# One matmul of 256 columns for the exponential sums of two heads, and one row buffer for six batches, in a fused attention and expert kernel

## The chip, the cores and the metric

The kernel runs on one core of a Trainium2 chip. A core has a matrix engine (TensorE; PE in the profile, PEld for its loads of stationary weights), a vector engine (VectorE, DVE), a scalar engine (ScalarE, ACT), a general engine (GpSimd, POOL) and an engine that starts transfers (SyncE, SP). They run side by side and wait for each other through semaphores. SBUF is the working memory, PSUM is where TensorE puts its products. The metric is the time of one execution in device microseconds (us).

## The reference

```
scores = scale * q @ k^T                        # 8 batches, 8 heads, 576 tokens, 64 per head
allowed = |i - j| <= 32, or i or j is one of 8 global tokens
attn = exp(scores - max), zero where not allowed
x = (attn / (sum(attn) + 1e-9)) @ v             # 4608 tokens of 512
logits = x @ w_gate                             # 8 experts
e = argmax(logits);  g = softmax(logits)[e]
out = g * (relu(x @ w1[e]) @ w2[e])             # w1 512x1024, w2 1024x512 for each expert
```

All values are fp32; the kernel multiplies fp16 values where it can and adds in fp32.

## The kernel before, in words

The attention part is a loop over 8 batches (`b`) of 6 stages (`t`), 48 in all, written out in full. A stage takes 48 keys of each half of the sequence (`f`, 0 and 1), and the 8 global keys, against the queries in their windows; a row of scores has 128 columns (`WE`). Heads come in 4 pairs (`c`), with a head `r` in each.

The order of the work is written by hand (a manual schedule): each engine executes its instructions in the order of the program. In a stage stand, in this order: transposes of the next batch's keys (`trans_qk`); `scores` of the next stage (L419 to L441) and their exponentials on ACT (`exps`, L445); a piece of the tail of the batch before; `pvs`, the products of exponentials with values (L456); transposes of the next queries; `zs`, the sums of exponentials (L461 to L471). `zs` multiplies a column selector `onesel` with the exponentials: for each of 2 heads, 4 pairs and 2 halves one fp32 matmul of 128 columns, the second head adding to the first in PSUM, in a different row of the same 32.

What is in PSUM is merged over the stages into `xt` (values) and `zt` (sums) by `merge` (L473 to L493): ACT copies the new columns (L486), DVE adds the overlapping ones (L491, or copies them at the first stage, L489). At a batch's end POOL joins the two halves (`join`, L501 to L506; DVE does it for the last batch), and `sum_globals` (L508 to L516) adds up the columns of global queries on POOL.

A `Tail` then turns a batch into routed rows. Its steps are spread over the stages of the next batch: `gate` multiplies `xt` by the gate's weights (L544) and adds the sums from `zt` into free rows of the same PSUM result, with a floor of 1e-30 (L548); `logits` transposes (L559), takes reciprocals of the sums and normalises (L564 to L571); `rows` transposes `xt` (L580) and multiplies it by the reciprocals into an fp16 row buffer `x16` (L581); `route1`, `ranks`, `route2` choose experts and slots; `exps` and `weights` write token numbers (L623, ACT) and gate weights (L659, DVE) to the last four columns of each row; `scatter` (L664) sends six groups of 108 rows from POOL, by indirect DMA, to slots in DRAM. The scatters of batch `b` are issued in batch `b + 2`, one after each stage. The row buffers are two, used by even and odd batches: one carved from the later home of the expert weights (`wall`), one a tile of its own (`x16x`).

At the top of batches 1 to 6 POOL also casts the next keys and queries (L328, eight casts), and fills global keys. During the last batch, rows of the first batches are gathered for the first two experts, whose first wave of matmuls (L769, L776) is interleaved with the last tail. The second part goes through the 8 experts with weights loaded through SP (L679), casts on ACT and DVE (L684, L686), and matmuls (L1155, L1176).

PSUM buffers named `tr` are two, shared by transposes, gates, logits and rows; `sc`, `pv` and `z` have one each.

Of the kernel before, what the change touches and what calls it, by code (L numbers as in the profile page):

```python
# [9 lines left out]
FP32 = mybir.dt.float32  # L10
FP16 = mybir.dt.float16
I32 = mybir.dt.int32
I16 = mybir.dt.int16
ALU = mybir.AluOpType
AF = mybir.ActivationFunctionType
AX = mybir.AxisListType
# [5 lines left out]
B, H, S, D = 8, 8, 576, 64  # L22
NG = 8
NTOK, DM, E, F = 4608, 512, 8, 1024
HW = 48
NSL = 12
NT = 6
KU = HW + NG
R = 6
WP = 20  # L30
WQ = R * WP
WE = WQ + NG
QP = 108
XP = 60
TB = 108
# [4 lines left out]
ROW = DM + 4  # L40
# [5 lines left out]
def kernel(  # L46
# [11 lines left out]
    nc = tc.nc  # L58
# [13 lines left out]
    def carve(parts, ncols, dt):  # L72
        n16 = ncols * (2 if dt is FP32 else 1)
        a = carve_at[0]
        carve_at[0] = a + (n16 + 15) // 16 * 16
        assert carve_at[0] <= 8 * 8192
        r = wflat[0:parts, a : a + n16]
        return r.bitcast(FP32) if dt is FP32 else r
# [4 lines left out]
    vb = [carve(128, NT * DM, FP32).rearrange("p (t n) -> p t n", t=NT) for _ in range(2)]  # L83
# [14 lines left out]
        r = stage[a // 1024][0:parts, a % 1024 : a % 1024 + n]  # L98
        return r.rearrange("p (a b) -> p a b", b=shape[1]) if len(shape) > 1 and parts == 128 else r

    x16b = [carve(TB, 6 * ROW, FP16).rearrange("p (j n) -> p j n", j=6)]

    att = ExitStack()
    ap_ = att.enter_context(tc.tile_pool(name="att", bufs=1))
# [3 lines left out]
    pvp = aps.enter_context(tc.tile_pool(name="ps_pv", bufs=1, space=PS))  # L108
    trp = aps.enter_context(tc.tile_pool(name="ps_tr", bufs=2, space=PS))

    x16b.append(ap_.tile([TB, 6, ROW], FP16, name="x16x"))

    xt = [ap_.tile([128, 2, 4, R + 1, XP], FP32, name=f"xt{i}") for i in range(2)]
    zt = [ap_.tile([128, 2, R + 1, XP], FP32, name=f"zt{i}") for i in range(2)]
    gsum = ap_.tile([128, 5, HW], FP32, name="gsum")
    xtg = ap_.tile([128, 5, B * NG], FP32, name="xtg")
    qt = [ap_.tile([128, 4, R, QP], FP16, name=f"qt{i}") for i in range(2)]
    kt = [ap_.tile([128, 4, NSL, 64], FP16, name=f"kt{i}") for i in range(2)]
    mask = carve(128, NSL * WE, FP16).rearrange("p (n w) -> p n w", n=NSL)
# [9 lines left out]
    id32 = sb.tile([128, 128], FP32, name="id32")  # L129
    idh = sb.tile([128, 128], FP16, name="idh")  # L130
    id2 = ap_.tile([128, 64], FP16, name="id2")
    onesel = ap_.tile([128, 2, 32], FP32, name="onesel")
    wgbd = ap_.tile([128, 4, 32], FP32, name="wgbd")
    ustr = ap_.tile([TB, 128], FP16, name="ustr")
    ones16 = ap_.tile([TB, 128], FP16, name="ones16")
# [132 lines left out]
    for a in (0, 64):  # L268
        s_ = slice(a, a + 64)
# [22 lines left out]
    for dst, src in ((kgh, k), (qgh, q)):  # L292
        for r in range(2):
# [4 lines left out]
                            in1=hsel.rearrange("p (h o) -> p h o", o=1).to_broadcast([64, H, 64]), op=ALU.mult)  # L298
# [14 lines left out]
    for eng, t0, t1 in ((nc.vector, 0, 1), (nc.gpsimd, 1, NT)):  # L313
        for f in range(2):
            ts = slice(NT * f + t0, NT * f + t1)
            eng.tensor_tensor(out=mask[:, ts, NG:WE], in0=m1o[:, :, NG:WE].to_broadcast([128, t1 - t0, WQ]),
                              in1=gk[:, ts].rearrange("p (n o) -> p n o", o=1).to_broadcast([128, t1 - t0, WQ]), op=ALU.add)
# [54 lines left out]
    for r in range(2):  # L372
        nc.sync.dma_start(
            out=wgbd[64 * r : 64 * r + 64, :, 8 * r : 8 * r + 8],
            in_=moe_w_gate.rearrange("(c r p) e -> r p c e", c=4, r=2)[r])
# [1 line left out]
    nc.vector.memset(qt[1][:, :, :, 102:108], 0.0)  # L377
    nc.vector.memset(kt[1][:, :, :, KU:64], 0.0)
    nc.vector.memset(onesel, 0.0)
    nc.vector.memset(onesel[:, 0, 16:17], 1.0)  # L380
    nc.vector.memset(onesel[:, 1, 17:18], 1.0)


    def routing_constants():
# [76 lines left out]
    def zs(b, t):  # L461
        e = eb[(NT * b + t) % 2]
        z = pvp.tile([128, 2, 512], FP32, tag="z", name="z")
        for r in range(2):
            for c in range(4):
                for f in range(2):
                    ff = slice(64 * f, 64 * f + KU)
                    nc.tensor.matmul(out=z[32 * c : 32 * c + 32, f, 0:WE],  # L468
                                     lhsT=onesel[ff, r, :], rhs=e[ff, r, c, :],
                                     start=(r == 0), stop=(r == 1))  # L470
        return z  # L471

    def merge(t, parts):  # L473

        o = 8 * t
        new, old = [], []
        for src, acc in parts:

            sn = bass.AP(src.tensor, src.offset, [list(src.ap[0]), list(src.ap[1]), [WP, R + 1], [1, 8]])
            new.append((acc[:, :, :, o + 12 : o + WP], sn))
            old.append((acc[:, :, 1 : R + 1, o : o + 12],
                        src[:, :, NG:WE].rearrange("p n (r a) -> p n r a", r=R)[:, :, :, 0:12]))
        def part(i):
            nc.scalar.activation(out=new[i][0], in_=new[i][1], func=AF.Copy)  # L486
            d_, s_ = old[-1 - i]
            if t == 0:
                nc.vector.tensor_copy(d_, s_)  # L489
            else:  # L490
                nc.vector.tensor_tensor(out=d_, in0=d_, in1=s_, op=ALU.add)  # L491

        return part  # L493

    def merge_x(b, t, pv):
        return merge(t, [(pv[:, f].rearrange("p (c w) -> p c w", c=4), xt[b % 2][:, f]) for f in range(2)])

    def merge_z(b, t, z):
        merge(t, [(z[:, :, 0:WE], zt[b % 2])])(0)

    def join(b, eng):  # L501
        x, z = xt[b % 2], zt[b % 2]
        for f, a0, a1 in ((0, 48, 0), (1, 6, 54)):
            for y in ((x[:, f, :, 1:, a0 : a0 + 6], x[:, 1 - f, :, 1:, a1 : a1 + 6]),
                      (z[:, f, 1:, a0 : a0 + 6], z[:, 1 - f, 1:, a1 : a1 + 6])):
                eng.tensor_tensor(out=y[0], in0=y[0], in1=y[1], op=ALU.add)  # L506

    def sum_globals(b):  # L508
        x, z = xt[b % 2], zt[b % 2]
        for y, g, d in ((x[:, :, :, 0, 12:XP], gsum[:, 0:4], xtg[:, 0:4]), (z[:, :, 0, 12:XP], gsum[:, 4], xtg[:, 4])):  # L510

            nc.gpsimd.tensor_tensor(out=g, in0=y[:, 0], in1=y[:, 1], op=ALU.add)
            for i, (n, m) in enumerate(((0, 24), (0, 8), (0, 16))):
                w = 24 if i == 0 else 8
                o = g[..., 0:w] if i < 2 else d[..., 8 * b : 8 * b + 8]
                nc.gpsimd.tensor_tensor(out=o, in0=g[..., 0:w], in1=g[..., m : m + w], op=ALU.add)  # L516
# [4 lines left out]
    class Tail:  # L521
        def __init__(self, b):
            self.b = b
            self.glob = b == B
            self.nj = 1 if self.glob else 6
            self.np = 64 if self.glob else TB
            self.lg = ap2.tile([TB, 6, 8], FP32, tag="lg", name="lg")
            self.rz = ap2.tile([TB, 6, 8], FP32, tag="rz", name="rz")
            self.x16 = x16b[b % 2]
            self.lsb = {}  # L530

        def xap(self, c, i):
            if self.glob:
                return xtg[:, c : c + 1, :]
            x = xt[self.b % 2][:, :, c] if c < 4 else zt[self.b % 2]
            o = (2 * i + 1) * XP + 6
            return x.rearrange("p f r a -> p f (r a)")[:, :, o : o + TB]

        def gate(self, i):
            nf = 1 if self.glob else 2  # L540
            n = nf * self.np
            ps = trp.tile([128, 512], FP32, tag="tr", name="tr_l")
            for c in range(4):
                nc.tensor.matmul(out=ps[32 * c : 32 * c + 32, 0:n].rearrange("p (f w) -> p f w", f=nf),  # L544
                                 lhsT=wgbd[:, c, :], rhs=self.xap(c, i), start=True, stop=True)
            l = ap2.tile([128, 2, TB], FP32, tag=f"lsb{i % 2}", name="lsb")

            nc.vector.scalar_tensor_tensor(out=l[:, 0:nf, 0 : self.np], in0=self.xap(4, i), scalar=1e-30,  # L548
                                           in1=ps[:, 0:n].rearrange("p (f w) -> p f w", f=nf),
                                           op0=ALU.max, op1=ALU.add)  # L550
            self.lsb[i] = l

        def logits(self, i):
# [234 lines left out]
    ps = trp.tile([128, 512], FP32, tag="tr", name="tr_v")  # L788
# [9 lines left out]
    for b in range(B):  # L798
# [9 lines left out]
        if b:  # L808
            sum_globals(b - 1)
# [3 lines left out]
        for t in range(NT):  # L813
            n = NT * b + t
# [13 lines left out]
            elif b + 1 == B:  # L828
# [6 lines left out]
                elif t == 5:  # L835
                    for i in range(2 * NW):
                        ps = trp.tile([128, 4, 128], FP16, tag="tr", name="tr_w")
# [36 lines left out]
            elif b + 1 == B and t == 1:  # L874
                tail.logits(1)
            mx(1)
            z = zs(b, t)
            merge_z(b, t, z)
            if b + 1 == B:
                if t == 0:  # L880
# [26 lines left out]
            elif t == 3:  # L907
                for s_ in range(2):
                    nc.sync.dma_start(out=vg.rearrange("p (u s r) d -> p u s (r d)", u=2, s=2)[8:64, :, s_],
                                      in_=vgr[64 * s_ + 8 : 64 * s_ + 64].rearrange("p (u r) d -> p u (r d)", u=2))  # L910
# [13 lines left out]
            if b + 1 == B and t < 2 * NW:  # L924
                gather(xr01[t], wi[:, t // 2, t % 2 : t % 2 + 1], scattered[0 : 6 * (B - 3)])
            if done is not None:
                done.scatter([t])
            if b + 1 == B and t >= 4:
                tail.scatter([t - 4])
            for _ in range(2 if n + 2 == NT * B else 1):  # L930
# [3 lines left out]
            if n >= NT * B - 18 and pre:  # L934
                staged.append((pre.pop(0), stage[len(pre) % 4]))
                wload(*staged[-1][0], staged[-1][1])
        join(b, nc.gpsimd if b + 1 < B else nc.vector)
        done = tail
        tail = Tail(b)
    tg = Tail(B)  # L940
    sum_globals(B - 1)
    assert not staged
    done.scatter([2, 3, 4, 5])
# [196 lines left out]
    for e in range(E):  # L1140
# [11 lines left out]
        for fb in range(8):  # L1152
            ps = psh.tile([128, 512], FP32, tag="h", name="h")[:, 0:N]
            for c in range(4):
                nc.tensor.matmul(out=ps, lhsT=w1v[:, e, c, 128 * fb : 128 * fb + 128], rhs=xts[:, c, 0:N],  # L1155
                                 start=(c == 0), stop=(c == 3))
# [3 lines left out]
            if fb % 2:  # L1160
                castp(nc.scalar if fb % 4 == 1 else nc.vector)
                j = fb // 2
# [10 lines left out]
        for j in range(NJ[e]):  # L1173
            ps = psy.tile([128, 512], FP32, tag="y", name="yp")
            for fc in range(8):
                nc.tensor.matmul(out=ps, lhsT=ht[:, fc, 128 * j : 128 * j + 128], rhs=w2v[:, e, fc, :],  # L1176
                                 start=(fc == 0), stop=(fc == 7))
# [111 lines left out]
```

## Time and profile before

| | us |
|---|---|
| median of 14 runs | 514.81 |
| lowest and highest | 508.63, 519.22 |
| the profiled execution | 517.26 |
| its span, first to last instruction | 515.5 |
| last z group of the attention part ends (span time) | 306.8 |

A line of a group reads: source line, engine, operation, what it writes from what, shape, count, then busy time, mean duration of one in ns, and idle time of the engine just before with what ended it. "Issue" means that the profile shows nothing that the engine waited for. In rows of a stretch, each engine has its busy time in us and, in brackets, how many instructions were in flight; the granted clock of TensorE, the busy share of the DMA engines and GB/s follow.

### The profile page before, as it was taken

Reading aid. Unit: us, or ns where it says so; the run is one execution under the profiler, and the core shown is the slowest. Engines: PE = TensorE matmul, PEld = TensorE weight load, DVE = VectorE, ACT = ScalarE, POOL = GpSimd, SP = SyncE. Lnnn points to the kernel's source line nnn. Section 1 sums busy time; section 2 is a strip of 40 time slices with the busy share of each in tenths; the row PEclk is TensorE's granted clock in tenths of the full one; section 3 lists DMA queues with packets and bytes.
Section 4 is the critical chain, followed back from the end, with each engine's and each line's share of the span. In section 5 each row is a group of like instructions: output and inputs, shape, how many; then the busy total and the mean of one; then the engine's idle time right before and its main releaser. Section 6 shows DMA issues by size and latency. Waiting matters only on the chain.

```text
span 515.5 us, 16371 instructions
## 1 busy us (share of the span) xinstructions
PE 419.7 (81%) x6661; PEld 260.1 (50%) x6661; DVE 253.8 (49%) x719; ACT 211.6 (41%) x385; POOL 241.3 (47%) x387
## 2 busy tenths in 40 slices
PE   3788779978797799797897857577989998999990
PEld 2456557746465476474574534345434444444450
DVE  6533445735355266376484427325775554333330
ACT  7234344523344155274472452234445544323330
POOL 7700370844806606518238134657436556543442
PEclk9999988978879779897598679879899999999997
DMA  8795979773914925947344201379989999221011
GB/s 200 107 212 104 218 159 186 157 169 55 245 46 102 207 49 111 301 135 168 118 126 138 67 24 39 102 253 308 355 246 364 368 366 368 92 79 59 20 42 57
DMA packets 119436, 84.06 MB, mean 163 GB/s; under 512 B 46552, under 2 KB 113880, under 8 KB 119356
## 3 DMA queue, kind: packets, MB, share of 16 engines
q1 hardware_dynamic: 110300, 63.57, 49.1%
q0 software_dynamic: 9056, 19.38, 11.4%
q8 instruction: 55, 0.90, 0.7%
q14 instruction: 25, 0.20, 0.1%
HBM read 68.51 MB, written 16.16 MB: 164 GB/s over the span
## 4 chain that ended last, share of the span: by engine, by line
PE 18%; issue 11%; DMA 9%; DVE 7%; POOL 5%; ACT 3%; another core or an unknown queue 1%; SPq 1%; POOLq 1%; DVEq 0%; ACTq 0%
DMA st<-in_moe_w_dram 6%; PE pv L456 3%; DMA xr<-xslot_scr,ovi 3%; PE yp L1176 3%; POOL xr L691 3%; POOL out_dram L720 2%; PE h L1155 2%; PE hp L769 2%; PE z L468 2%; PE tr_x L580 2%; PE yw L776 1%; ACT wall L684 1%; SPq L679 1%; DVE xt L491 1%
## 5 line engine op out<-in xcount | busy, mean ns | idle before, releaser
L456 PE MATMUL pv<-wall 56*64 56x128 f32 x1536 | 84.5, 323 | 15.3 <-issue 14.1
L456 PEld LDWEIGHTS pv<-wall 56*64 56x64 f32 x1536 | 59.3, 160 | 35.4 <-issue 30.9
L445 ACT ACTIVATE wall<-sc 128x1024 f32<-128x1024 f32 x48 | 49.1, 1023 | 64.0 <-remote 40.4
L506 POOL TENSOR_TENSOR xt<-xt 128x144 f32<-128x144 f32 x14 | 7.1, 506 | 130.4 <-DVE xt L491 130.4
L491 DVE TENSOR_TENSOR xt<-xt,pv 128x288 f32<-128x288 f32 x80 | 36.3, 453 | 62.8 <-ACT xt L486 61.3
L486 ACT ACTIVATE xt<-pv 128x224 f32<-128x224 f32 x96 | 34.3, 357 | 72.1 <-PE pv L456 30.1
L1155 PE MATMUL h<-xts,wall 128*128 128x512 f16 (+1 forms) x256 | 54.1, 354 | 8.7 <-issue 4.9
L1176 PE MATMUL yp<-wall,ht 128*128 128x512 f16 x224 | 51.1, 385 | 0.7 <-DVE ht L733 0.5
L468 PE MATMUL z<-wall,onesel 56*32 56x128 f32 x1536 | 41.9, 312 | 3.8 <-issue 3.7
L720 POOL DMA_INDIRECT out_dram<-y,xr x24 | 25.2, 1052 | 35.4 <-DVE y L717 23.2
L1155 PEld LDWEIGHTS <-wall 128*128 128x128 f16 x256 | 24.3, 98 | 29.9 <-issue 9.3
L328 POOL CAST wall<-wall 96x768 f16<-96x768 f32 (+1 forms) x48 | 37.3, 821 | 0.0
L438 PEld LDWEIGHTS <-kt 64*64 64x64 f16 x1536 | 28.6, 123 | 14.0 <-issue 10.7
L1176 PEld LDWEIGHTS <-ht 128*128 128x128 f16 x224 | 21.8, 99 | 26.6 <-issue 1.5
L580 PE MATMUL tr_x<-id,xt 128*108 128x128 f32 x192 | 32.1, 297 | 3.5 <-DVE x16x L581 1.8
L684 ACT ACTIVATE wall<-st 128x1024 f16<-128x1024 f32 x24 | 25.3, 1053 | 20.7 <-DMA st<-in_moe_w_dram 14.2
L664 POOL DMA_INDIRECT xslot_scr<-wall,si x25 | 24.8, 992 | 18.6 <-ACT wall L445 10.0
L468 PEld LDWEIGHTS z<-wall,onesel 56*32 56x32 f32 x1536 | 23.9, 119 | 16.4 <-issue 12.3
L438 PE MATMUL sc<-qt,kt 64*64 64x120 f16 x768 | 28.4, 238 | 3.5 <-issue 3.5
L733 DVE TENSOR_SCALAR ht<-h 128x512 f16<-128x512 f32 (+1 forms) x32 | 19.9, 622 | 22.3 <-PE h L1155 19.7
L691 POOL DMA_INDIRECT xr<-xslot_scr,idx x24 | 25.4, 1057 | 9.6 <-issue 6.5
L664 POOL DMA_INDIRECT xslot_scr<-x16x,si x24 | 23.9, 996 | 12.4 <-issue 10.6
(270 smaller groups left out, 744.3 us busy)
## 6 DMA issues: line engine op xcount, KB each, us to landing
st<-in_moe_w_dram SPq DMA_DIRECT2D x96, 256.0 KB
wall<-in_v_dram SPq DMA_DIRECT2D x96, 96.0 KB
wall<-in_moe_w_dram SPq DMA_DIRECT2D x32, 256.0 KB
wall<-in_k_dram SPq DMA_DIRECT2D x42, 192.0 KB
wall<-in_q_dram SPq DMA_DIRECT2D x42, 192.0 KB
wall<-vg SPq DMA_DIRECT2D x14, 96.0 KB
wall<-in_k_dram SPq DMA_DIRECT2D x4, 288.0 KB
wall<-in_q_dram SPq DMA_DIRECT2D x4, 288.0 KB
```

Source lines behind the costliest of these rows:

```text
L328: eng.tensor_copy(o, i_)
L438: nc.tensor.matmul(out=o[:, NG:WE].rearrange("p (r a) -> p r a", r=R) if part == 0 else o[:, 0:NG], lhsT=kt[b % 2][rr, c, sl, :], rhs=rhs, ...
L445: nc.scalar.activation(out=e.rearrange("p r c w -> p r (c w)"), in_=sc[:, :, 0 : 4 * WE], func=AF.Exp, scale=0.125)
L456: nc.tensor.matmul(out=pv[64 * r : 64 * r + 64, f, c * WE : (c + 1) * WE], lhsT=vt[ff, t, 64 * h : 64 * h + 64], rhs=e[ff, r, c, :], start ...
L468: nc.tensor.matmul(out=z[32 * c : 32 * c + 32, f, 0:WE], lhsT=onesel[ff, r, :], rhs=e[ff, r, c, :], start=(r == 0), stop=(r == 1))
L491: nc.vector.tensor_tensor(out=d_, in0=d_, in1=s_, op=ALU.add)
L580: nc.tensor.transpose(out=ps[p, 128 * c : 128 * c + 128], in_=src, identity=id32)
L664: d_ = nc.gpsimd.indirect_dma_start(out=xslot, out_offset=IndirectOffsetOnAxis(ap=self.si[p, j : j + 1], axis=0), in_=self.x16[p, j, :].bi ...
L691: d_ = nc.gpsimd.indirect_dma_start(out=xr.bitcast(I16), out_offset=None, in_=xslot, in_offset=IndirectOffsetOnAxis(ap=ix, axis=0), bounds ...
L720: d_ = nc.gpsimd.indirect_dma_start(out=out, out_offset=IndirectOffsetOnAxis(ap=xr[:, DM : DM + 2].bitcast(I32), axis=0), in_=y, in_offset ...
L1155: nc.tensor.matmul(out=ps, lhsT=w1v[:, e, c, 128 * fb : 128 * fb + 128], rhs=xts[:, c, 0:N], start=(c == 0), stop=(c == 3))
L1176: nc.tensor.matmul(out=ps, lhsT=ht[:, fc, 128 * j : 128 * j + 128], rhs=w2v[:, e, fc, :], start=(fc == 0), stop=(fc == 7))
```

## The change

Sums: `zs` has 8 matmuls instead of 16, each over both heads of a pair, 256 columns; `onesel` has ones in both rows 16 and 17, so that both rows get the sums of both heads, each head in columns of its own. `zt`, `gsum` and `xtg` get a dimension for the head. The merge, the join and the sum of globals take both. The gate picks the row that belongs to a head with a mask of rows, `rowsel`, one fused multiply and add for each head; the floor of 1e-30 moves from the gate to the merge.

Row buffers: batches 0 to 5 and 7 share the carved one; batch 6 and the global tokens use the buffer of values that batch 6 leaves free; `x16x` is gone. In batches before the last, the six scatters come after the first four stages.

```diff
-    x16b = [carve(TB, 6 * ROW, FP16).rearrange("p (j n) -> p j n", j=6)]
+    x16b = [carve(TB, 6 * ROW, FP16).rearrange("p (j n) -> p j n", j=6)] * B
+    v16 = vb[B % 2].rearrange("p t n -> p (t n)").bitcast(FP16)[0:TB]
+    x16b[B - 2] = v16[:, 0 : 6 * ROW].rearrange("p (j n) -> p j n", j=6)
+    x16b.append(v16[:, 6 * ROW : 7 * ROW].rearrange("p (j n) -> p j n", j=1))
...
-    x16b.append(ap_.tile([TB, 6, ROW], FP16, name="x16x"))
...
-    zt = [ap_.tile([128, 2, R + 1, XP], FP32, name=f"zt{i}") for i in range(2)]
-    gsum = ap_.tile([128, 5, HW], FP32, name="gsum")
-    xtg = ap_.tile([128, 5, B * NG], FP32, name="xtg")
+    zt = [ap_.tile([128, 2, 2, R + 1, XP], FP32, name=f"zt{i}") for i in range(2)]
+    gsum = ap_.tile([128, 6, HW], FP32, name="gsum")
+    xtg = ap_.tile([128, 6, B * NG], FP32, name="xtg")
...
-    nc.vector.memset(onesel[:, 0, 16:17], 1.0)
-    nc.vector.memset(onesel[:, 1, 17:18], 1.0)
+    nc.vector.memset(onesel[:, 16:18], 1.0)
+
+    for r in range(2):
+        nc.vector.tensor_reduce(out=rowsel[:, r : r + 1], in_=id32.rearrange("p (c n) -> p c n", c=4)[:, :, 16 + r],
+                                op=ALU.add, axis=AX.X)
...
-        for r in range(2):
-            for c in range(4):
-                for f in range(2):
-                    ff = slice(64 * f, 64 * f + KU)
-                    nc.tensor.matmul(out=z[32 * c : 32 * c + 32, f, 0:WE],
-                                     lhsT=onesel[ff, r, :], rhs=e[ff, r, c, :],
-                                     start=(r == 0), stop=(r == 1))
+        for c in range(4):
+            for f in range(2):
+                ff = slice(64 * f, 64 * f + KU)
+                nc.tensor.matmul(out=z[32 * c : 32 * c + 32, f].rearrange("p (r w) -> p r w", r=2)[:, :, 0:WE],
+                                 lhsT=onesel[ff], rhs=e[ff, :, c, :], start=True, stop=True)
...
-            nc.scalar.activation(out=new[i][0], in_=new[i][1], func=AF.Copy)
+            nc.scalar.activation(out=new[i][0], in_=new[i][1], func=AF.Copy, bias=floor)
             d_, s_ = old[-1 - i]
-            if t == 0:
+            if t == 0 and floor:
+                nc.vector.tensor_single_scalar(out=d_, in_=s_, scalar=floor, op=ALU.add)
+            elif t == 0:
                 nc.vector.tensor_copy(d_, s_)
...
-        merge(t, [(z[:, :, 0:WE], zt[b % 2])])(0)
+        merge(t, [(z.rearrange("p f (r w) -> p (f r) w", r=2)[:, :, 0:WE],
+                   zt[b % 2].rearrange("p f r n a -> p (f r) n a"))], 1e-30)(0)
...
-                      (z[:, f, 1:, a0 : a0 + 6], z[:, 1 - f, 1:, a1 : a1 + 6])):
+                      (z[:, f, :, 1:, a0 : a0 + 6], z[:, 1 - f, :, 1:, a1 : a1 + 6])):
...
-            nc.vector.scalar_tensor_tensor(out=l[:, 0:nf, 0 : self.np], in0=self.xap(4, i), scalar=1e-30,
-                                           in1=ps[:, 0:n].rearrange("p (f w) -> p f w", f=nf),
-                                           op0=ALU.max, op1=ALU.add)
+            lv = l[:, 0:nf, 0 : self.np]
+            for r in range(2):
+                nc.vector.scalar_tensor_tensor(out=lv, in0=self.xap(4 + r, i), scalar=rowsel[:, r : r + 1],
+                                               in1=lv if r else ps[:, 0:n].rearrange("p (f w) -> p f w", f=nf),
+                                               op0=ALU.mult, op1=ALU.add)
...
-                done.scatter([t])
+                done.scatter([t] if b + 1 == B else ((0,), (1, 2), (3, 4), (5,), (), ())[t])
```

More of the change, by code (lines that the diff above doesn't have):

```diff
@@ L131 @@
     id2 = ap_.tile([128, 64], FP16, name="id2")
-    onesel = ap_.tile([128, 2, 32], FP32, name="onesel")
+    onesel = ap_.tile([128, 32], FP32, name="onesel")
+    rowsel = ap_.tile([128, 2], FP32, name="rowsel")
     wgbd = ap_.tile([128, 4, 32], FP32, name="wgbd")
@@ L463, in zs, with merge @@
         z = pvp.tile([128, 2, 512], FP32, tag="z", name="z")
-        for r in range(2):
-            for c in range(4):
-                for f in range(2):
-                    ff = slice(64 * f, 64 * f + KU)
-                    nc.tensor.matmul(out=z[32 * c : 32 * c + 32, f, 0:WE],
-                                     lhsT=onesel[ff, r, :], rhs=e[ff, r, c, :],
-                                     start=(r == 0), stop=(r == 1))
+        for c in range(4):
[3 more added lines that the diff above has]
+                                 lhsT=onesel[ff], rhs=e[ff, :, c, :], start=True, stop=True)
         return z
-    def merge(t, parts):
+    def merge(t, parts, floor=0.0):
         o = 8 * t
@@ L509, in sum_globals @@
         x, z = xt[b % 2], zt[b % 2]
-        for y, g, d in ((x[:, :, :, 0, 12:XP], gsum[:, 0:4], xtg[:, 0:4]), (z[:, :, 0, 12:XP], gsum[:, 4], xtg[:, 4])):
+        for y, g, d in ((x[:, :, :, 0, 12:XP], gsum[:, 0:4], xtg[:, 0:4]), (z[:, :, :, 0, 12:XP], gsum[:, 4:6], xtg[:, 4:6])):
             nc.gpsimd.tensor_tensor(out=g, in0=y[:, 0], in1=y[:, 1], op=ALU.add)
@@ L528, in __init__ @@
             self.rz = ap2.tile([TB, 6, 8], FP32, tag="rz", name="rz")
-            self.x16 = x16b[b % 2]
+            self.x16 = x16b[b]
             self.lsb = {}
@@ L534, in xap @@
                 return xtg[:, c : c + 1, :]
-            x = xt[self.b % 2][:, :, c] if c < 4 else zt[self.b % 2]
+            x = xt[self.b % 2][:, :, c] if c < 4 else zt[self.b % 2][:, :, c - 4]
             o = (2 * i + 1) * XP + 6
```

## The prediction

> **What bounds the kernel now.** I read the page first, then the groups with their shapes kept apart, then busy time by stretches, then the timeline of single stages. The page has TensorE (PE) busy for most of the span:
>
> ```profile
> PE 419.7 (81%) x6661; PEld 260.1 (50%) x6661; DVE 253.8 (49%) x719; ACT 211.6 (41%) x385; POOL 241.3 (47%) x387
> ```
>
> That share mixes three regimes of the attention part (0 to 307 us), which the stretches keep apart (columns: PE, weight load, DVE, ACT, POOL, granted clock, DMA share, GB/s):
>
> ```profile
> 98.00:102.00 4.00, 3.91 (x140) 2.83 (x118) 3.30 (x11) 2.54 (x5) 3.61 (x10) 1.00 1.02 249
> 105.00:110.00 5.00, 2.51 (x21) 1.28 (x20) 0.00 (x0) 0.95 (x1) 3.78 (x5) 0.85 1.13 252
> 196.00:200.00 4.00, 4.00 (x120) 2.96 (x124) 3.13 (x9) 2.11 (x5) 2.75 (x6) 1.00 0.43 76
> 210.00:215.00 5.00, 2.53 (x21) 1.13 (x20) 0.00 (x0) 0.00 (x0) 3.96 (x4) 0.93 1.16 290
> 282.00:287.00 5.00, 2.67 (x13) 0.83 (x14) 0.00 (x0) 0.00 (x0) 3.06 (x4) 0.50 0.30 84
> ```
>
> Normal stages take about 4 us (from one L468 group to the next in the timeline: 191.36, 195.28, 199.20, 203.29, 207.27), with 120 to 140 matmuls in 4 us: PE is the bound there. The rows with 13 to 21 matmuls in 5 us are the second regime: POOL issues six row scatters (L664) one after another, 1.3 us apart, and PE trickles without any semaphore being named. It costs about 7 us in each of batches 2 to 6 and more in batch 7, and lasts as long as POOL's scatters do (208.73 to 216.22 in batch 5; PE is back at 217.4). The third is batch 0, where PE waits for DVE's casts.
>
> What is to change stands in these groups (line, engine, operation, names, shape, count | busy us, mean ns | idle before):
>
> ```profile
> L468 PE MATMUL z<-wall,onesel 56*32 56x128 f32 x1536 | 41.9, 312 | 3.8 <-issue 3.7
> ...
> L486 ACT ACTIVATE zt<-z 128x112 f32<-128x112 f32 x48 | 12.5, 260 | 10.1 <-remote 6.5 <-PE z L468 3.5
> L491 DVE TENSOR_TENSOR zt<-zt,z 128x144 f32<-128x144 f32 x40 | 11.9, 298 | 7.9 <-ACT zt L486 4.6 <-issue 3.3
> ...
> L548 DVE SCALAR_TENSOR_TENSOR lsb<-zt,tr_l 128x216 f32<-128x216 f32 x24 | 8.9, 373 | 10.2 <-PE tr_l L544 10.2
> ```
>
> How matmuls of one such group follow each other is seen by cutting one group of 32 into four slices; the count beside PE is of matmuls in flight in the slice (columns: PE, weight load, DVE, ACT, clock, DMA, GB/s):
>
> ```profile
> 199.19:199.30 0.11, 0.10 (x8) 0.10 (x16) 0.00 (x0) 0.00 (x0) 1.00 0.17 19
> 199.32:199.41 0.09, 0.09 (x16) 0.09 (x21) 0.00 (x0) 0.00 (x0) 1.00 0.21 23
> 199.43:199.52 0.09, 0.09 (x24) 0.09 (x16) 0.00 (x0) 0.00 (x0) 1.00 0.21 23
> 199.54:199.63 0.09, 0.09 (x25) 0.06 (x8) 0.00 (x0) 0.00 (x0) 1.00 0.21 23
> ```
>
> Eight start together (eight corners of the array: two row halves, four column strips), then eight more about every 0.11 us: four rounds, two heads times the two passes that a fp32 product takes here. Within a round starts are 7 ns apart, so a round is set by its 128 columns, not by the number of instructions. The same stage on the other engines:
>
> ```profile
> 199.20 0.67 PE L468 MATMUL z<-wall,onesel 56*32 56x128 f32 x32
> ...
> 199.67 0.37 DVE L548 SCALAR_TENSOR_TENSOR lsb<-zt,tr_l 128x216 f32<-128x216 f32 x1
> ...
> 200.55 0.30 DVE L489 COPY zt<-z 128x144 f32<-128x144 f32 x1
> ...
> 200.76 0.37 DVE L548 SCALAR_TENSOR_TENSOR lsb<-zt,tr_l 128x216 f32<-128x216 f32 x1
> ...
> 201.31 0.39 PE L544 MATMUL tr_l<-xt,wgbd 128*32 128x216 f32 x4
> ```
>
> **The change, part by part.**
>
> *Z matmuls.* Per stage 16 fp32 products of 128 columns become 8 of 256; in records 32 become 16, and 1536 of 13,322 PE records (matmuls and weight loads) disappear. The columns streamed through each corner are the same: four rounds of 0.11 us become two of 0.21 to 0.22 us (L544 shows it: 216 columns, second pass 0.21 us after the first). The last instruction starts earlier and lasts about 0.11 us longer, so the group still takes about 0.66 against 0.67 us. I take 0. From both sides: all the overhead of the three round changes gone, 0.03 us x 48 = -1.4 us; no overlap between the two wider rounds, 0.03 x 48 = +1.4 us. [...]
>
> *PE's supply of instructions.* Fewer instructions help where PE is starved. In batch 7 the z group itself lies in a scatter stretch (279.5 to 287.7): 64 records in 8.2 us. The stretch ends with POOL, so the saved slots only let PE do some 30 later instructions early, worth about 0.4 us at normal speed. PE also stops once for 2.6 us in the middle of L438 (163.8 to 166.4) with no wait named, while a 16 KB packet of the instruction queue arrives; all such stops on L438 add to 6.3 us, longest 2.6. A tenth fewer instructions: 0.6 us. Together -1.0; bounds -6.3 (none left) and +2.6 (they fall elsewhere, one more long one).
>
> *Evacuation of z.* ACT's copy goes from 112 to 224 elements: the row for that size is L486 xt, 357 ns, +0.10 us; DVE's from 144 to 288: L491 xt, 453 ns, +0.155 us. Times 48 that is 4.7 us of ACT and 7.4 us of DVE. ACT's (41% busy) is covered by PE's stage, except in batch 0; without the cover it costs up to 4.7. DVE's lands on PE in two places. Batch 0: PE waits for a DVE cast in four stages, and that cast stands behind zt, which stands behind ACT's zt: 4 x 0.25 = +1.0. In batches 1 to 6, the transpose group L580 at 193.67 waits 0.3 us for DVE's row product (L581), which stands behind zt: 6 x 0.155 = +0.9. Elsewhere DVE has about a quarter of each normal stage free (3.13 of 4.00 busy); if not, 48 x 0.155 = 7.4. [...]
>
> *Gate.* One fused operation becomes two, the second waiting for the first. Price of the second: 373 ns by L548 itself; its operands are all in SBUF, where L506 on DVE (144 elements) plus 72 elements at L491's slope gives 375; with 35 ns between dependent operations 0.41 us, x 24 = 9.8 us, plus 0.25 for the global tail (its row is 209 ns). The tr buffer is released by the first of the two. In the timeline above the next gate's matmul (201.31) needs the buffer that L548 releases at 201.13: with a second operation and a longer zt ahead of it, less 0.14 us idle, that moves by some 0.4, slack 0.18: about +0.2 in each of batches 1 to 6, +1.2. In batch 7 gates and logits stand close together (268 to 276, DVE nearly always busy, PE waits for `tmp`): +0.8. In the last tail (309.8 to 316) DVE gets up to 0.86 us late but PE's interleaved expert matmuls cover most: +0.4. Bound: all on the path, 10.1.
>
> *POOL.* The z part of the join grows from 36 to 72 elements (262 ns; between that and 506 for 144, about 343), twice, and of the global sums by about 0.2: scatters start 0.35 us later per batch. PE is then starved later by as much and no longer: 0, at most 5 x 0.35 = 1.8.
>
> *One row buffer.* Scatters 1 to 5 stand earlier in POOL's program (after stages 0 to 3 rather than 0 to 5), six indirect DMAs as before, past no other POOL work in batches 2 to 6 and past nothing on SP. POOL reaches them late anyway (208.7, when PE is in stage 2), so they issue at the same times. New waits: DVE's row products in stage 3 for scatter 0, ACT's token write L623 in stage 4 for all six; behind the first DVE's merges queue, behind the second ACT's next exponentials, and PE behind both. In batch 5 the last scatter is issued by 216.2 and its queue is empty at 220.1; ACT comes to L623 at 224.7. Margin 4.6 us: cost 0. Rows in `wall` also make L623 wait for DVE (3 waits, 3.2 us; none in x16x) and now do so in each batch; stages with it are as long as those without (3.93, 3.92): 0, at most 3 x 1.05. The row mask (two small reductions for one memset less) lies in the setup, under loads: 0, at most 0.5.
>
> Sum: 0 - 1.0 + 1.0 + 0.9 + 1.2 + 0.8 + 0.4 = +3.3 us. The profiled execution took 517.26 us (span 515.5) and would be 520.6; the median of the 14 runs is 514.81, which makes 518.1.
>
> **The rivals.**
> A, faster: the starved stretches cost per instruction and not per scatter. Then batch 7's z group loses half of its 8.2 us (-4.1), the 2.6 us stop goes, and half of the DVE cost hides (+2.2): 514.8 - 4.5 = 510.3. For it: matmuls at a steady 4 per us there. Against: PE recovers within about 1.5 us of POOL's last scatter, in every batch.
> B, no change: DVE's idle quarter takes all of it; +4.3 goes, -1.0 stays: 513.8. For it: PE is rarely seen waiting for DVE. Against: the two places where it is.
> C, much slower: the single buffer makes ACT wait in stage 4. It decides once POOL is 4.6 us later than now; at 6 us it costs 1.4 in each of five batches, 518.1 + 7 = 525. For it: POOL is a chain from the join through eight casts. Against: 0.35 us is all that is added.
> That the change saves PE nothing is part of my forecast.
>
> **How the numbers follow.** Forecast 0.56, own range 515.5 to 520.5; A 0.16; B 0.18; C 0.10. About 0.5% (2.6 us) is what a measurement of this kernel can tell: faster is under 512.2, slower over 517.4. Faster: nearly all of A, 0.16. Slower: two thirds of the forecast (0.38) and C, 0.48. Within: B and the rest, 0.36. The range reaches from the upper part of A to the lower part of C, 511.5 to 523.5.
>
> **What would show it.** Right: L468 with 768 records, one group still 0.6 to 0.7 us; ACT zt near 357 and DVE zt near 453 ns; two L548-like operations near 370; normal stages 4.0 to 4.2 us, longer in stages 1 and 5; scatter stretches as long as before. Wrong: z groups near 0.4 us (the columns do not bind), shorter scatter stretches (A), ACT waiting for a scatter's DMA in stage 4 (C).

## The result, and the profile after

The changed kernel takes **532.93 us** (median of 10 runs, 522.59 to 538.3) against 514.78 us for the kernel before beside it (47 runs), 18 us more. The ratio, 1.023 (95% interval 1.018 to 1.028) or 12 us, compares only the fast runs of each kernel, those within 1.5% of its fastest. So it is slower, as forecast, but by 12 to 18 us and not by 3.3, and above the upper end of the range. The profiled execution has a span of 529.8 us against 515.5.

The page of the changed kernel, busy time by engine:

```profile
PE 423.7 (80%) x5893; PEld 248.6 (47%) x5893; DVE 284.1 (54%) x745; ACT 215.5 (41%) x385; POOL 247.7 (47%) x387
```

PE has 768 records fewer and is no less busy; ACT has 4 us more, POOL 6 us more and DVE 30 us more. The groups of the changed kernel, shapes apart (busy us, mean ns | idle before), say where these 30 us are:

```profile
L474 PE MATMUL z<-wall,onesel 56*32 56x256 f32 x768 | 40.3, 469 | 0.3 <-issue 0.2
...
L558 DVE SCALAR_TENSOR_TENSOR lsb<-zt,rowsel,lsb 128x216 f32<-128x216 f32 x24 | 24.5, 1021 | 0.8
...
L499 DVE TENSOR_TENSOR zt<-zt,z 128x288 f32<-128x288 f32 x40 | 18.0, 450 | 15.3 <-ACT zt L492 12.2 <-issue 3.0
...
L492 ACT ACTIVATE zt<-z 128x224 f32<-128x224 f32 x48 | 17.0, 354 | 17.1 <-remote 9.3 <-PE z L474 6.2 <-PE tr_qk L345 1.2
...
L558 DVE SCALAR_TENSOR_TENSOR lsb<-zt,rowsel,tr_l 128x216 f32<-128x216 f32 x24 | 10.3, 429 | 1.8 <-PE tr_l L553 1.7
```

The sums (L474) and their evacuation (L492, L499) cost what the prediction says. The surprise is the second operation at the gate, the one whose two tensor inputs are `zt` and `lsb`: 1021 ns in the mean, where 0.41 us was priced. The same line of the trace by itself shows that this is no mean of equal pieces (ns min/median/max, first and last start), and who waited for it (us, times):

```profile
L558 DVE SCALAR_TENSOR_TENSOR lsb<-zt,rowsel,tr_l x24: 421/428/440, 63.6 to 326.0; 128x216 f32<-128x216 f32 x24
L558 DVE SCALAR_TENSOR_TENSOR lsb<-zt,rowsel,lsb x24: 444/556/3127, 64.1 to 326.5; 128x216 f32<-128x216 f32 x24
...
  PE tr_l L553: 11.7, 5
```

The first operation, which reads `tr_l` from PSUM, is the same everywhere. The second is 444 ns where it is short and 3127 ns where it is long. The timeline of batch 5 (start us, us) shows what lies beside a long one:

```profile
204.27 5.59 POOL L332 CAST wall<-wall 96x768 f16<-96x768 f32 x7
...
205.09 0.43 DVE L558 SCALAR_TENSOR_TENSOR lsb<-zt,rowsel,tr_l 128x216 f32<-128x216 f32 x1
...
205.55 2.85 DVE L558 SCALAR_TENSOR_TENSOR lsb<-zt,rowsel,lsb 128x216 f32<-128x216 f32 x1
...
208.32 0.44 DVE L497 COPY xt<-pv 128x288 f32<-128x288 f32 x1
208.69 0.44 DVE L495 TENSOR_SCALAR zt<-z 128x288 f32<-128x288 f32 x1
...
209.06 0.42 DVE L558 SCALAR_TENSOR_TENSOR lsb<-zt,rowsel,tr_l 128x216 f32<-128x216 f32 x1
```

POOL runs its casts of the next batch's queries and keys back to back, and the operation lasts until five of them are over. Behind it on DVE stand the merge of `xt`, that of `zt` and the next gate's first operation, and PE waits 2.73 us for a `tr` buffer. The stretches of the changed kernel (length, then PE, weight load, DVE, ACT, POOL, granted clock, DMA share, GB/s) show what this costs PE:

```profile
205.00:207.00 2.00, 1.80 (x66) 0.95 (x50) 1.96 (x3) 1.32 (x4) 2.00 (x4) 1.00 0.39 45
207.00:209.00 2.00, 0.00 (x0) 0.00 (x0) 2.00 (x3) 0.96 (x1) 2.00 (x3) 0.86 0.48 137
209.00:211.00 2.00, 1.47 (x20) 0.79 (x24) 1.50 (x4) 0.00 (x0) 2.00 (x4) 0.50 1.02 272
211.00:213.00 2.00, 2.00 (x34) 1.55 (x26) 0.56 (x2) 0.36 (x1) 1.76 (x6) 0.50 1.15 248
213.00:215.00 2.00, 2.00 (x26) 1.05 (x24) 1.48 (x4) 0.71 (x2) 1.15 (x6) 0.50 1.18 248
```

The kernel before, in the same stages of its own batch 5:

```profile
205.00:207.00 2.00, 1.91 (x73) 1.46 (x62) 1.73 (x6) 1.41 (x3) 1.76 (x6) 1.00 1.15 243
207.00:209.00 2.00, 2.00 (x66) 1.39 (x67) 1.56 (x5) 1.15 (x4) 1.13 (x5) 1.00 1.20 237
```

After the change PE does nothing from 207 to 209 us, and then the clock granted to it is half until 215: 20 to 34 matmuls in 2 us instead of 66 to 73 at full clock. Stage 1 of batch 5, with a stall of 2.7 us in it, is 4.8 us longer than before; whether the stall brought the lower clock was not tried.

Stage lengths, read from the end of one group of sums to the end of the next in the timeline, in us. "One op" and "PSUM" are two experiments below, in their first profiles:

| stage 1 of batch | before | one op | PSUM | after |
|---|---|---|---|---|
| 2 | 4.09 | 4.17 | 5.36 | 6.89 |
| 3 | 4.24 | 4.21 | 5.10 | 4.83 |
| 4 | 8.46 | 4.44 | 5.16 | 8.90 |
| 5 | 4.09 | 4.17 | 5.06 | 8.90 |
| 6 | 4.09 | 4.21 | 4.70 | 6.94 |
| 7 | 4.02 | 4.07 | 4.97 | 4.39 |
| attention part done at | 306.8 | 304.8 | 302.8 | 320.5 |

In batches 2, 4, 5 and 6 PE waits 2.7 to 2.8 us for L558. From batch end to batch end, batch 2 is 3.4 us longer than before, batch 5 5.8 us (granted clock 0.50 from 209 to 215 us) and batch 6 2.9 us. Batch 4 is no longer, since the kernel before has a stop of its own in that stage; in batch 3 the gate comes late in the series of casts and waits 0.7 us. With 2.3 us of batch 0, and less 0.6 us in the others, that makes the 13.7 us by which the attention part ends later; the rest of the program is about as long as before (209.3 against 208.7 us).

The rows that could have told this stand in the trace of the kernel before. Its plan of waves (L748 to L761) has small DVE operations with two inputs in SBUF, and they fall beside the casts of batch 6 (timeline of the kernel before):

```profile
230.92 5.45 POOL L328 CAST wall<-wall 96x768 f16<-96x768 f32 x7
...
233.16 1.67 DVE L748 SCALAR_TENSOR_TENSOR bw<-base,ebasef 128x2 f32<-128x2 f32 x1
234.76 0.85 DVE L750 TENSOR_TENSOR idw<-ofs,ebasef 128x4 f32<-128x4 f32 x1
235.64 0.74 DVE L753 TENSOR_TENSOR w__4712<-idw,bw 128x4 f32<-128x4 f32 x1
```

Two elements take 1.67 us. No wait names these operations, and they are in no list of costly groups. They are not free, though: on DVE the third gate's L548 stands behind the plan and begins only at 238.57, and PE waits for it (us in total, times, longest):

```profile
PE tr_lt L559 <- DVE lsb L548: 2.9, 1, 2.9
```

How much of this wait ends up in the time of the kernel before was not tried.

### The profile page after: what moved, and what is told of

Read it like the earlier page. It is cut to its first block, busy times and chain, and to the rows that moved or that the text cites. A ratio compares the mean times of both kernels' runs of the same rounds, so it can differ in the third digit from the quotient of the medians.

```text
span 529.8 us, 14865 instructions
## 1 busy us (share of the span) xinstructions
PE 423.7 (80%) x5893; PEld 248.6 (47%) x5893; DVE 284.1 (54%) x745; ACT 215.5 (41%) x385; POOL 247.7 (47%) x387
## 5 line engine op out<-in xcount | busy, mean ns | idle before, releaser
L463 PE MATMUL pv<-wall 56*64 56x128 f32 x1536 | 81.8, 325 | 12.9 <-issue 11.2
L452 ACT ACTIVATE wall<-sc 128x1024 f32<-128x1024 f32 x48 | 49.0, 1021 | 53.5 <-remote 29.7
L492 ACT ACTIVATE xt<-pv 128x224 f32<-128x224 f32 x96 | 34.3, 357 | 79.7 <-PE pv L463 41.9
L499 DVE TENSOR_TENSOR xt<-xt,pv 128x288 f32<-128x288 f32 x80 | 36.2, 453 | 51.0 <-ACT xt L492 48.0
L674 POOL DMA_INDIRECT xslot_scr<-wall,si x49 | 48.7, 994 | 30.1 <-issue 19.7
L591 DVE TENSOR_TENSOR wall<-tr_x,rz 108x512 f16<-108x512 f32 (+1 forms) x49 | 33.5, 687 | 20.8 <-PE tr_x L590 15.4
L474 PE MATMUL z<-wall,onesel 56*32 56x256 f32 x768 | 40.3, 469 | 0.3 <-issue 0.2
L445 PEld LDWEIGHTS <-kt 64*64 64x64 f16 x1536 | 30.3, 124 | 20.6 <-issue 17.4
L332 POOL CAST wall<-wall 96x768 f16<-96x768 f32 (+1 forms) x48 | 38.9, 853 | 0.0
L590 PE MATMUL tr_x<-id,xt 128*108 128x128 f32 x192 | 33.6, 306 | 5.2 <-DVE wall L591 3.1
L445 PE MATMUL sc<-qt,kt 64*64 64x120 f16 x768 | 30.8, 240 | 5.6 <-issue 5.6
L445 PE MATMUL sc<-qgt,kt 64*64 64x8 f16 x768 | 26.8, 180 | 5.9 <-issue 5.9
L350 ACT ACTIVATE kt<-tr_qk 128x576 f16<-128x576 f16 x32 | 20.8, 650 | 21.9 <-PE tr_qk L345 16.0
```

The costliest lines, as they stand in the source:

```text
L332: eng.tensor_copy(o, i_)
L445: nc.tensor.matmul(out=o[:, NG:WE].rearrange("p (r a) -> p r a", r=R) if part == 0 else o[:, 0:NG], lhsT=kt[b % 2][rr, c, sl, :], rhs=rhs, ...
L452: nc.scalar.activation(out=e.rearrange("p r c w -> p r (c w)"), in_=sc[:, :, 0 : 4 * WE], func=AF.Exp, scale=0.125)
L463: nc.tensor.matmul(out=pv[64 * r : 64 * r + 64, f, c * WE : (c + 1) * WE], lhsT=vt[ff, t, 64 * h : 64 * h + 64], rhs=e[ff, r, c, :], start ...
L474: nc.tensor.matmul(out=z[32 * c : 32 * c + 32, f].rearrange("p (r w) -> p r w", r=2)[:, :, 0:WE], lhsT=onesel[ff], rhs=e[ff, :, c, :], sta ...
L590: nc.tensor.transpose(out=ps[p, 128 * c : 128 * c + 128], in_=src, identity=id32)
```

## The experiments

Theory 1: the second operation waits for POOL's casts because both its tensor inputs lie in SBUF. Theory 2: the one row buffer makes an engine wait. Theory 3: the longer evacuation of `z` on DVE. Theory 4: an operation with a column of row picks as its scalar is slow by itself.

**The result between the two operations kept in PSUM.** The changed kernel with

```diff
-                nc.vector.scalar_tensor_tensor(out=lv, in0=self.xap(4 + r, i), scalar=rowsel[:, r : r + 1],
-                                               in1=lv if r else ps[...],
+                nc.vector.scalar_tensor_tensor(out=lv if r else ps_view, in0=self.xap(4 + r, i),
+                                               scalar=rowsel[:, r : r + 1], in1=ps_view,
                                                op0=ALU.mult, op1=ALU.add)
```

> Theory 1 (the gate's second operation, whose two tensor operands both lie in SBUF, waits for POOL's casts): here the first operation writes its sum back into the PSUM tile and the second reads it there, so each operation has one operand in SBUF and one in PSUM. The second takes 420 to 450 ns in every batch, beside the casts too, PE no longer waits 2.7 us for it, and the time is 517 to 519 us (+2.5 to +4 on the kernel before). Theory 2 (the one row buffer makes an engine wait) and theory 3 (the longer evacuation of z on DVE): as slow as the changed kernel, 529 to 533 us. Theory 4 (an operation with a scalar from a column of row picks is slow by itself): the second stays above 1 us in mean, 529 us or more.

Measured: 517.16 us (median of 10 runs) against 517.85 for the kernel before in the same set of runs, ratio 0.995, interval 0.987 to 1.003. The time is in the expected range; the +2.5 to +4 us on the kernel before are not there. The attention part is done at 302.8 us. The operations, by line (ns min/median/max; the profile is of the same kernel's third set of runs, the ladder below):

```profile
L559 DVE SCALAR_TENSOR_TENSOR tr_l<-zt,rowsel,tr_l x24: 434/439/448, 62.2 to 312.7; 128x216 f32<-128x216 f32 x24
L559 DVE SCALAR_TENSOR_TENSOR lsb<-zt,rowsel,tr_l x24: 440/440/441, 62.7 to 313.2; 128x216 f32<-128x216 f32 x24
```

440 ns at every gate, with the same casts beside them, the same scalar column, the same evacuation and the same row buffer. Theories 2, 3 and 4 can't be the cause of the large loss. What a second operation costs when nothing blocks it is seen in who PE waits for (us in total, times, longest), in the same profile:

```profile
PE tr_l L553 <- DVE lsb L559: 2.5, 5, 0.5
...
PE tr_qk L345 <- DVE lsb L559: 1.7, 4, 0.6
```

**One operation at the gate.** The changed kernel with a column that picks both rows, applied to head 0's sums:

```diff
-            for r in range(2):
-                nc.vector.scalar_tensor_tensor(out=lv, in0=self.xap(4 + r, i), scalar=rowsel[:, r : r + 1], ...
+            nc.vector.scalar_tensor_tensor(out=lv, in0=self.xap(4, i), scalar=rowboth, in1=ps[...],
+                                           op0=ALU.mult, op1=ALU.add)
```

> The changed kernel with one operation at the gate, whose column picks both rows: head 1 of each pair is divided by the sums of head 0, so this part of the computation is changed. Theory 1: what is left of the change is the evacuation of z on ACT and DVE, batch 0 and stage 5: 515.5 to 517.5 us (+1 to +2.5). Theories 2 and 3: 527 to 533 us, since row buffer and evacuation are as in the changed kernel.

Measured: 515.9 us (4 runs, 510.38 to 519.79) against 517.85: inside the expected range of times, though not above the kernel before. Its stages 1 are 4.07 to 4.21 us, apart from batch 4: the evacuation costs next to nothing there.

**Only the second operation, added to the kernel before.**

```diff
                                            op0=ALU.max, op1=ALU.add)
+            nc.vector.scalar_tensor_tensor(out=lv, in0=self.xap(4, i), scalar=zcol, in1=lv,
+                                           op0=ALU.mult, op1=ALU.add)
```

> The kernel before with only a second operation at the gate added, which adds zero times the sums to its result, both operands in SBUF. Theory 1: it takes about 2.85 us at the first gate of batches 1, 2, 4, 5 and 6 and 0.44 where POOL does not cast; 526 to 530 us (+11 to +15). Theories 2 and 3: +0.5 to +3 us, 515.5 to 518 us, with the second operation near 0.45 us or its length harmless.

Measured: 524.92 us (4 runs), +7.1 us, ratio 1.014, interval 1.004 to 1.024. The added operation:

```profile
L554 DVE SCALAR_TENSOR_TENSOR lsb<-zt,zcol,lsb x24: 444/594/2876, 59.9 to 319.0; 128x216 f32<-128x216 f32 x24
```

The same long operations appear, 2.5 to 2.9 us in batches 2, 4, 5 and 6 (1.5 us in batch 1), in a kernel that has nothing else of the change. The loss is about half of what I expected: PE's waits are 2.1 to 2.5 us, and batches 3 and 4 came out shorter. The duration is shown; how much of it ends up in the total depends on what else stops PE in that stage.

**Only the one row buffer, on the kernel before**: `x16b` as one carved tile for batches 0 to 5, `self.x16 = x16b[b]`, and the scatters in the order of the change.

> The kernel before with only the one row buffer for six batches and its order of scatters. Theory 1: 0 +- 1.5 us, 513.5 to 516.5 us. Theory 2: most of the loss, 524 to 530 us. Theory 3: no change.

Measured: 514.66 us (10 runs) against 517.85, ratio 0.988, interval 0.982 to 0.994. Not slower, so theory 2 falls as the cause of most of the loss, but an interval below 1 was unexpected; it was timed again, with the PSUM form:

> The kernel before with only the one row buffer, timed once more in more rounds, since its first interval lay below 1 while its traced attention part was no shorter (305.6 against 306.8 us). If the buffer alone saves time: a ratio of 0.985 to 0.995 again. If the first interval was the spread of the runs: 0.995 to 1.005.

> The changed kernel with the gate's first result kept in PSUM, in more rounds. If nothing of the loss is left once the second operation no longer meets POOL's casts: ratio 0.99 to 1.00. If the rest of the change costs the +1 to +4 us that my sum gives it: 1.002 to 1.008.

Measured: 516.79 us (12 runs) and 517.55 us (6 runs) against 512.36; ratios 1.006 (1.001 to 1.011) and 1.011 (1.003 to 1.018). The gain did not come back; both ratios lie above all that was expected of them (1.005 and 1.008 at most).

**POOL writes but does not read.** The question is whether POOL's reading makes the operation wait, or any instruction on POOL. The changed kernel, casts of batches 2 to 7 replaced:

```diff
-                cast_qk(pair, nc.gpsimd, nc.gpsimd)
+                for src in (kf, qf):
+                    nc.gpsimd.memset(src[:, 768 * pair : 768 * pair + 768], 0.0)
```

> The changed kernel, with POOL's casts of batches 2 to 7 replaced by memsets of the same extent on the casts' sources: POOL writes to SBUF and reads nothing. The casts are left out, so those batches work with the queries and keys of batch 1. [...]

Measured, the second operation (ns min/median/max):

```profile
L558 DVE SCALAR_TENSOR_TENSOR lsb<-zt,rowsel,lsb x24: 443/444/790, 66.1 to 311.4; 128x216 f32<-128x216 f32 x24
```

The timeline of batch 5 (start us, us) has the first two gates:

```profile
197.15 5.50 POOL L815 MEMSET wall<- 96x768 f32 x8
...
198.45 0.44 DVE L558 SCALAR_TENSOR_TENSOR lsb<-zt,rowsel,lsb 128x216 f32<-128x216 f32 x1
...
200.01 0.77 DVE L558 SCALAR_TENSOR_TENSOR lsb<-zt,rowsel,lsb 128x216 f32<-128x216 f32 x1
```

POOL is as busy in that place (eight memsets of 733 ns, casts took about 820), and the operation takes 0.44 us at the first gate of each of batches 1 to 6, beside the memsets, where beside casts it took 2.84 to 3.13 in five of the six batches. So the long wait was there where POOL read and wrote, and not where it only wrote. At one later gate in each of batches 1 to 5 it takes 0.57 to 0.79 us, in batch 3 when the memsets are over; this rest of 0.1 to 0.35 us was not explained. The attention part is done at 304.6 us instead of 320.5. The total of the one run, 522.57 us, says nothing: what follows the attention part is 216 us long instead of 209, and it was anything from 206 to 216 us in the profiles of this document.

Nor does the operation wait for the running cast alone: in batch 5 of the changed kernel it arrives at 205.55, during the second cast, and three more begin (205.81, 206.58, 207.35) before the time at which it can have started, its end (208.40) less the 0.44 us of an undisturbed one.

**Casts cut in two**: each cast of POOL as two of 384 elements per partition. The question is whether the operation waits for a number of casts, for a fixed time or for the whole series.

> The changed kernel, each of POOL's casts cut into two of half the size (about 0.4 us apart instead of 0.77). [...]

Measured: 528.4 us (one run); the attention part is done at 310.4 us instead of 320.5, and the rest is 216 us long. The second operation, and the timeline of batch 5 (start us, us):

```profile
L561 DVE SCALAR_TENSOR_TENSOR lsb<-zt,rowsel,lsb x24: 443/444/3883, 61.5 to 317.7; 128x216 f32<-128x216 f32 x24
```

```profile
204.63 4.00 POOL L331 CAST wall<-wall 96x384 f16<-96x384 f32 x8
...
205.48 1.24 DVE L561 SCALAR_TENSOR_TENSOR lsb<-zt,rowsel,lsb 128x216 f32<-128x216 f32 x1
...
207.83 0.44 DVE L561 SCALAR_TENSOR_TENSOR lsb<-zt,rowsel,lsb 128x216 f32<-128x216 f32 x1
```

At the first gates of batches 2, 4, 5 and 6 it takes 1.23 to 1.31 us, where it took 2.84 to 2.91 beside whole casts. Its start can be estimated as its end less the 0.44 us of an undisturbed one. Counted in casts: with whole casts it arrives during the second and starts before the sixth, in all five long cases of the profile above; arriving during the seventh it starts before the eighth. With half casts it arrives during the third and starts before the sixth, in all five cases. So it does not wait for a fixed time, nor just for the running cast. But no count of casts holds throughout. With the operation added to the kernel before, and in the change's second profile (the ladder below), it got in before the fourth cast in batch 1, behind which POOL paused; in that second profile another that arrived during the fifth cast took 2.85 us, until the series was over. With half casts, operations that arrive during the tenth or eleventh take 3.4 and 3.9 us in batches 1 and 3, until the series is over, where others that arrive during the eighth or tenth take 0.44 us. Why it gets in at one place of the series and not at another stays open.

**The ladder.** Since the small steps had come out on both sides of 1, four kernels were run side by side:

> First rung of a ladder on one chip, since two earlier calls put the same kernels on both sides of 1: the kernel before with the one row buffer alone. The buffer is free: ratio to the kernel before 0.995 to 1.005.

> Second rung: the changed kernel with one operation at the gate (head 1 divided by the sums of head 0, so part of the computation is changed). By my sum the longer evacuation of z costs +1.9 and the shorter program saves 1.0: ratio 1.000 to 1.005 (515 to 517 us on a chip where the kernel before takes 514.8).

> Third rung: both operations at the gate, with the result between them in PSUM. The second operation without POOL in its way: +0.8 us in stage 1 of batches 2 to 7 by the traces, so 3 to 5 us above the second rung, ratio 1.004 to 1.012.

> Last rung: the changed kernel, second operation with both operands in SBUF. If the wait for POOL's casts is the cause, this rung is the high one: 9 to 14 us above the third, ratio 1.020 to 1.030.

| kernel | median us (6 runs each; before 11) | ratio | interval |
|---|---|---|---|
| before | 511.16 | | |
| one row buffer alone | 516.26 | 1.012 | 1.005 to 1.019 |
| change, one operation at the gate | 517.51 | 1.015 | 1.008 to 1.021 |
| change, PSUM between the operations | 520.91 | 1.018 | 1.010 to 1.026 |
| change | 536.48 | 1.052 | 1.043 to 1.060 |

All four ratios lie above what was expected of them. The last rung is 15.6 us, somewhat more than I expected, and is the one between 440 ns and up to 3 us for the second operation; its interval is clear of the others. The rung from one to two operations is 3.4 us, but the intervals of the first three rungs overlap. The first rung contradicts the first timing of the same kernel (0.988). Over the three sets of runs, each on another chip, the one-buffer kernel's medians are 514.7, 516.8 and 516.3, those of the kernel before 517.9, 512.4 and 511.2: it is the kernel before that moved more. The sign of the buffer's own effect is not settled; its three ratios run from 0.988 to 1.012. The change loses 25 us here and 12 to 18 us in its first runs, while the attention part ends at 320.6 and 320.5 us in the two profiles; what makes this difference was not found. No wait in the one-buffer kernel's trace names a scatter. ACT waits more often for the row product than before (3.2 us in three waits there):

```profile
ACT wall L625 <- DVE wall L583: 5.5, 6, 1.1
```

No form beat the kernel before in all its timings.

## Why the prediction was right or wrong

**Z matmuls, 0: right.** A group takes 0.66 us against 0.67; the 256 columns bind, and half the instructions saved next to nothing: all groups together are busy for 40.3 us against 41.9.

**PE's supply, -1.0: not shown.** In batch 7 the group of sums fell from 8.2 to 2.4 us (5.0 in the PSUM form, with as few instructions), and the batch as a whole only from 42.4 to 42.0, as the prediction has it (0.4). The stop of 2.6 us in batch 4 is gone in the first profiles of the PSUM and one-operation forms (stage of 5.16 and 4.44 us), but not in the second one of the one-operation form (7.79), and it is gone in one profile of the one-buffer kernel (4.88), which has all the old instructions. So the shorter program can't be given the credit.

**Evacuation, +1.9: sizes right.** ACT 354 ns (357 said), DVE 450 ns (453). In batches 2 to 4 stage 5 became 4.07 or 4.08 us from 3.92, the 0.15 of the prediction; in batch 5 it is 3.88 from 3.93. Batch 0 can't be read: it ended between 53.8 and 62.7 us in the profiles, which is wider than the +1.0.

**Gate, +2.4 with a bound of 10.1: this is the step that failed.** "Price of the second: 373 ns by L548 itself; its operands are all in SBUF, where L506 on DVE (144 elements) plus 72 elements at L491's slope gives 375." L548 reads one input from PSUM, and L506 runs on DVE only after the last batch, when POOL casts nothing; neither row had both the operation's inputs and its neighbours. The operation takes up to 3.1 us beside POOL's casts, 24.5 us of DVE in place of 9.8, and PE stands idle 11.7 us for it. The bound was none, since it multiplied a price taken where nobody disturbs. The row that has both, two SBUF inputs beside casts, was L748 at 1.67 us. So the failed step is that the price left out the wait for POOL. What the runs show in place of the 2.4 us is the ladder's last rung, 15.6 us between an operation that waits for the casts and one that does not. A smaller miss: "+0.2 in each of batches 1 to 6" was low even for an undisturbed second operation. The PSUM form has stages 1 that are 0.5 to 1.2 us longer than the one-operation form, and 3.4 us of total in the ladder, where the intervals overlap; it also holds the `tr` buffer for both operations, which the change does not. The first operation rose too, from 373 to 429 ns.

**POOL, 0: nearly right.** In each batch with a long operation two casts take 970 ns instead of 820, in batch 5 the sixth and the eighth, beside which the second operations of the first two gates end.

**One row buffer, 0:** no scatter is waited for, so the margin of the prediction held; its effect on the total, 0.988 to 1.012, is open.

**The sum.** All terms but the gate's wait for POOL are in the PSUM form. Over its three sets of runs it has a median of 517.65 us (22 runs), and the kernel before in the same sets 514.59 (47 runs): +3.1 against +3.3. But the single sets say -0.7, +5.2 and +9.8, so that the pooled figure comes out so close is luck; two of the three intervals lie above 1, and no more than the order of size is confirmed.

**The rivals.** A is out: PE was not sped up. B is out: DVE was full just where it mattered (busy for 2.00 of 2.00 us from 207 to 209 in batch 5). C had the sign and 10 of the 12 to 18 us, but its mechanism, ACT waiting in stage 4 for a scatter, does not occur. None of the four cases asked what POOL does beside the new operation, and so the range ended at 523.5.

## What to carry to other kernels

Price a new DVE operation by a row with the same inputs in the same memories and the same neighbour on POOL; its shape alone is not enough. Before a second operation on SBUF alone is added, look at what POOL reads during it, and keep one of the inputs in PSUM where that is possible: here that is one changed operand, 440 ns in place of up to 3127. And look for tiny operations with absurd durations in the profile before: here it was two elements in 1.67 us.

## What was not expected of the hardware

- A DVE operation with both inputs in SBUF took 2.85 us and let three more casts of POOL begin before it started (the start taken as its end less 0.44 us), although it had arrived before them; with casts of half the size it waited 0.8 us, and in two cases 2.9 to 3.4 us. Beside memsets of the same extent it lost nothing at the first gates and at most 0.35 us at later ones.
- After PE's 2.7 us of idleness the granted clock stood at 0.50 for some 6 us in batch 5 (209 to 215 us); that stage took 8.9 us, and in batch 6, after a wait as long (2.8 us), 6.9 us. In the change's second profile the clock fell to 0.50 after such a wait in batch 2 too, whose stage 1 took 8.2 us. What decides between the two, and whether the idleness itself lowers the clock, was not tried.
- The same kernel before had medians of 511.2, 512.4, 514.8 and 517.9 us in four sets of runs. Steps of about 1% were not settled by the interval of a single set of runs.
